# A list scheduler that counts TensorE's instruction blocks and spaces its transfers

## The chip, the cores and the metric

One core of one Trainium2 chip. The metric is the device time of one launch in microseconds, the median of several runs; the kernel before takes 421.56 us (three runs, 420.73 to 422.47).

## The reference, cut to what matters

Attention with a window of 96 keys and 8 global keys, and on its result, transposed to tokens by 512, a feed-forward block with a spatial gate:

```python
scores = scale * np.matmul(q, k.transpose(0, 1, 3, 2))      # 4 x 8 heads, 768 x 768, head size 64
scores = np.where(keep, scores + bias, -1000000000.0)       # bias falls with distance, by head
a = np.exp(scores - np.max(scores, axis=-1, keepdims=True))
attn = np.matmul(a / (np.sum(a, axis=-1, keepdims=True) + 1e-09), v)
...
h = gelu(x @ w_in)                                          # x: 4 x 768 x 512, w_in: 512 x 1024
u, v = h[..., :512], h[..., 512:]
v_n = (v - mu) / np.sqrt(var + 1e-06) * g_ln
v_s = np.einsum('ts,bsd->btd', w_sg, v_n) + b_sg[None, :, None]
out = x + (u * v_s) @ w_out
```

## The kernel before

Attention is cut into 48 units: a batch, a pair of heads, and one of three pairs of 128-query tiles. Of a unit, `score` (L794) multiplies q by the keys in reach in products of 64 x 64 quarters of TensorE, `softmax` takes the minimum on VectorE (L825) and the exponential on ScalarE (L830), and a turn brings the weights to the layout that the product with v needs. For units 0 to 15 the turn is made on TensorE (`turn_quarters`, L929), into two PSUM banks (`tps`) which ScalarE or VectorE copies to `pt` (L937, L938). From unit 16 on VectorE turns blocks of 32 (L893) and two transfers through DRAM do the rest (`far<-tt` L901, four issues; `pt<-far` L905). `weigh` (L959) multiplies by v. A quarter product in float32 is recorded as two passes, so one row of the order with x20 stands for 40 matmuls of the trace.

The feed-forward block works in split float32: a number is the sum of a high and a low part, and each product is three dense matmuls (L466, L467, L468) of 128 x 128 weights by 384 or 512 columns: v tiles (`mm_ps<-win,x`), u tiles (`mm_ps<-x,win`), the spatial mix (`mm_ps<-wsg,z`) and the output (`mm_ps<-gt,wout`). The weights come as 64-bit floats and are split on the fly: a transfer to `stage` (L628), a scaling on ScalarE (L631), bit operations on VectorE (L634, L636, L638), a cast (L641) and a difference (L643). All eight PSUM banks are one pool that scores, turns and dense products share.

What stands in which order on the engines is not written by hand. Every step is recorded as an `Op` with a duration for each engine that can do it, the buffers it uses and the steps it follows. `Plan.search` draws 40 sets of rules and shifts, `Plan.order` walks through time with each of them (an engine that is free takes the first step that is ready, by due time; TensorE by the order in which the code names the steps, up to 40 steps ahead), and the set whose modelled end is earliest is emitted. Every engine then runs its instructions in that order, whatever the real times are. A transfer is modelled as a single wire: it begins 1.3 us after its issue or when the wire is free, takes its bytes, and lands `LANDS` later; no transfer is issued in the plan while the wire is booked more than 1.8 us ahead.

Until 29 us of planned time `keep_on` (L415) puts matmuls on zeros ("fillers") where the plan has TensorE wait for 0.6 us or more.

Of the kernel before, what the change touches and what calls it, by code (L numbers as in the profile page):

```python
# [34 lines left out]
AHEAD = 3  # L35
# [30 lines left out]
PAIRS = 20  # L66
# [29 lines left out]

SLACK = 0.6

LANDS = 1.5

QUEUED = 1.8

# [23 lines left out]
    return "POOL_TS", 0.05 + n / 390 + more, 0.08 + n / 390 + more  # L126


def on_pe(busy, quarters=False):
    return "PE", busy, busy + 0.17, quarters  # L130


class Buf:

    def __init__(self, make, kind=None, spare=0):
        self.spare = spare
# [30 lines left out]
class Op:  # L169
# [2 lines left out]

    def __init__(self, ways, number):
        self.number = number
        self.quarters = ways[0][3] if ways[0][0] == "PE" else None
# [6 lines left out]
        self.ready, self.left, self.due = 0.0, 0, None  # L182


class Now:
# [13 lines left out]
class Plan:  # L199
# [9 lines left out]
    def op(self, ways, reads=(), writes=(), after=()):  # L209
        o = Op(ways, len(self.ops))  # L210
        o.before.update(after)
        for used, put in ((reads, False), (writes, True)):
            for b, part in parts(used):
                o.ready = max(o.ready, b.since)
                for other, at, puts in b.uses:
                    if other is not o and (put or puts) and (None in (part, at) or part == at):
                        o.before.add(other)
                b.uses.append((o, part, put))
                if b not in o.bufs:
                    o.bufs.append(b)  # L220
                    b.ops.append(o)
        self.ops.append(o)
        return o
# [54 lines left out]
    def order(self, start, rules, pace):  # L278
# [7 lines left out]
                b.placed = False  # L286
        free = {e: start.get(e, 0.0) for e in self.ENGINES}
        wire, mode = 0.0, False

        held = {"DVE": 0.0, "POOL": 0.0}  # L290

# [36 lines left out]
        while len(done) < len(self.ops):  # L328
            went = False
            for e in self.ENGINES:  # L330
                if free[e] > t:
                    continue

                short = set()
                can = [o for o in sorted(wait[e], key=pe_at.get if e == "PE" else due)
                       if o.ready <= t and not (o.dma and wire > t + QUEUED)
                       and room(o, e, short)]
                if e == "PE":
                    while head < len(pe) and pe[head].begin is not None:
                        head += 1  # L340
                    can = [o for o in can if pe_at[o] - head <= self.AHEAD]
                    first = pe[head] if head < len(pe) else None
                    if first and first not in can and not first.left and first.ready <= t + 0.12:
                        can = [] if room(first, e, set()) else can
                for o in can:
                    if (e == "SP" and firsts(o) and head < len(pe)
                            and o.due > max(pe[head].due, 0.0) + early):
                        continue
                    way = next(w for w in o.ways if w[0] == e)
                    if begin(way) > t + 0.1:  # L350
                        continue
# [12 lines left out]
                for w in o.ways:  # L364
                    wait[w[0]].remove(o)
                more = 0.0
                if e == "PE":
                    more, mode = self.switch(mode, o.quarters), o.quarters
                    if pace and o.begin > pace[taken] + LAG:
                        return done, math.inf  # L370
                    taken += 1
                free[e] = o.begin + way[1] + more
                o.end = o.begin + way[2] + more
                if way[3]:
                    held[e] = free[e]
                if o.dma:
                    wire = max(wire, t + 1.3) + way[2]
                    o.end = wire + LANDS
                done.append(o)
                for b in firsts(o):  # L380
                    at = places[b.kind]
                    b.slot = min((i for i, x in enumerate(at) if x is not None), key=at.__getitem__)
                    o.since = max(o.since, at[b.slot])
                    at[b.slot], b.placed = None, True
                for b in o.bufs:
                    if b.kind and all(x.begin is not None for x in b.ops):
                        places[b.kind][b.slot] = max(x.end for x in b.ops)
                for x in o.after:
                    x.left -= 1
                    x.ready = max(x.ready, free[e] if e == x.ways[0][0] == "PE" else  # L390
                                  o.end + (SYNC if x.ways[0][0] != e else -0.08))
                    if not x.left:
                        open_for(x)
            if not went:
                nexts = [f for f in [wire - QUEUED, *free.values(), *held.values()] if f > t] + [
                    x + more for at in places.values() for x in at if x is not None
                    for more in (0.0, SLACK) if x + more > t] + [
                    o.ready for e in self.ENGINES for o in wait[e] if o.ready > t]
                if not nexts:
                    return done, math.inf  # L400
                t = min(nexts) + 1e-6
        return done, max(o.end for o in done)

    def keep_on(self, o):

        to = next((b for b in o.bufs if b.kind == "bank" and b.ops[0] is o), None)
        gap = o.begin - o.since
        if to is None or gap < IDLE or o.begin > ON_UNTIL:
            return
        first = o.since == 0.0  # L410

        n = to.ap.shape[1]
        for _ in range(int((gap - 1.0) / (0.000844 * n) if first else
                           (gap - 0.25) / (0.000417 * n + 0.007))):
# [28 lines left out]
class Moe:  # L443
# [13 lines left out]
    def terms(self, n, cols, parts, reads, behind, after, ahead=None):  # L457
# [12 lines left out]
        def add(i):  # L470
            read = reads(i)
            if i == 0:
                read = [r for a in range(n - behind) for r in reads(a)]
            first = self.plan.op([on_pe(3 * cols * 0.000453) + (partial(put, i),)], read, [ps])
            if i == 0 and ahead:
                ahead(first)
            if i == n - 1:
                after(ps)
# [170 lines left out]
def local_global_attention_moe(tc, qk_in, v_in, q_t, k_t, v_n, n_gl, w_in, g_ln, w_sg_t, b_sg,  # L649
# [108 lines left out]

    def bank(name, n, spare=0):
        return Buf(lambda i: pp.tile([P, FF], F32, tag=f"bank{i}", name=name)[:, 0:n], "bank",  # L760
                   spare if scored < PAIRS + AHEAD else min(spare, SPARE_LATE))

    def build_bias(j):
        for h in (2 * j, 2 * j + 1):
# [21 lines left out]
    def score(n, after):  # L786
# [126 lines left out]
    def turn_quarters(n):  # L913
# [19 lines left out]
        turns[:] = [op([on_pe(0.117 * nt, True) + (put,)], ps + [diag], tps)]  # L933
# [7 lines left out]
    def weigh(ns):  # L941
# [56 lines left out]
        first = op([on_pe((0.36 if u == 0 else 0.48) * len(ns), True) + (put,)], used, av)  # L998

        def rest(between):  # L1000

            free = op([(e, 0.06, 0.12, partial(guard, eng)) for e, eng in (
                ("ACT", nc.scalar), ("DVE", nc.vector), ("POOL_TS", nc.gpsimd))], (), (), [first])
            op([on_pe(0.242 * len(ns), True) + (again,)], used, av, between + [free])
            return av

        return first, rest
# [388 lines left out]
```

## Time and profile before

| | |
|---|---|
| median of three runs | 421.56 us (420.73 to 422.47) |
| span of the profiled execution, first to last instruction | 420.1 us |
| TensorE busy | 403.7 us, 96%, 5224 matmuls and 5224 weight loads |
| VectorE / ScalarE / GpSimd busy | 323.5 / 228.2 / 174.6 us |
| TensorE, 5.72 to 57 us: matmuls, share of time busy | 1338, 88% |
| TensorE, 130 to 415 us | 2950, 99.8% |
| instruction transfers (queue 8) | 43, 0.70 MB together |

The page gives the span of the profiled execution and not its device time; the median of the runs stands 1.46 us above that span. A row of the trace gives what an engine ran, how long, and in brackets how long the engine had been idle and what ended that wait. "issue" is a wait that nothing in the profile explains. Busy TensorE is modelled from the starts of matmuls, which overlap.

### The profile page before, as it was taken

The page shows a single profiled execution, that of the slowest core. Times are in us where ns is not written, and L with a number is a line of the kernel's source. Part 1 is how long each engine was busy: PE and PEld are TensorE (multiplying, and loading weights), DVE is VectorE, ACT ScalarE, POOL GpSimd, SP SyncE. Part 2 cuts the span into 40 slices and gives each one's busy share as a digit, 9 for nine tenths or more (in the row PEclk, how much of TensorE's full clock was granted, in tenths as well). Part 3 has the DMA queues.
Part 4 walks back from the last instruction along what each step waited for, and adds up shares of the span by engine and source line. Part 5 has one row for each costly group of instructions (what it writes and reads, how often), then busy time and mean ns, then how long its engine had stood idle before and what let it go on. Part 6 is the DMA issues. An engine that isn't in the chain of part 4 may idle for free.

```text
span 420.1 us, 13632 instructions
## 1 busy us (share of the span) xinstructions
PE 403.7 (96%) x5224; PEld 368.2 (88%) x5224; DVE 323.5 (77%) x1037; ACT 228.2 (54%) x744; POOL 174.6 (42%) x306
## 2 busy tenths in 40 slices
PE   8888989999999999999999999999999999999994
PEld 5766867899998889799999989999999888999994
DVE  6787989999997699995777899885768578754362
ACT  5898889765765765753356556653255343311220
POOL 2234447365686646353554355442553122303100
PEclk9999999989999999999999999999999999999998
DMA  7666575526877778754798785562886521001002
GB/s 246 201 208 166 154 238 153 158 81 173 240 249 255 192 228 238 208 162 114 211 271 227 226 240 141 155 170 54 244 281 172 152 85 39 2 2 48 29 0 81
DMA packets 50040, 68.20 MB, mean 162 GB/s; under 512 B 5809, under 2 KB 33969, under 8 KB 49969
## 3 DMA queue, kind: packets, MB, share of 16 engines
q1 hardware_dynamic: 49968, 67.26, 54.7%
q8 instruction: 43, 0.70, 0.8%
q14 instruction: 29, 0.23, 0.2%
HBM read 48.89 MB, written 18.35 MB: 160 GB/s over the span
## 4 chain that ended last, share of the span: by engine, by line
PE 79%; ACT 6%; DVE 5%; DMA 4%; issue 3%; POOL 1%; SPq 1%; DVEq 0%; POOLq 0%; ACTq 0%
PE mm_ps L466 22%; PE mm_ps L467 21%; PE mm_ps L468 21%; PE s_ps L794 6%; PE av L959 6%; PE tps L929 2%; ACT p L830 2%; DMA pt<-far 2%; DMA qk<-in_qk_in_dram 1%; DMA far<-tt 1%; DVE p L825 1%; DMA v<-in_v_in_dram 1%; ACT stage L631 1%; ACT wsg L641 1%; ACT pt L937 0%
## 5 line engine op out<-in xcount | busy, mean ns | idle before, releaser
L830 ACT ACTIVATE p<-p,pst 128x192 f32<-128x192 f32 (+1 forms) x192 | 84.0, 440 | 36.8 <-DVE pst L825 34.9
L466 PE MATMUL mm_ps<-wsg,z 128*128 128x384 f32 x192 | 65.5, 341 | 0.1
L467 PE MATMUL mm_ps<-wsg,z 128*128 128x384 f32 x192 | 64.9, 338 | 0.0
L468 PE MATMUL mm_ps<-wsg,z 128*128 128x384 f32 x192 | 64.8, 338 | 0.0
L825 DVE CUSTOM_DVE_ANT_0 p<-s_ps,bias 128x192 f32<-128x192 f32 (+1 forms) x192 | 56.5, 337 | 5.1 <-PE s_ps L794 4.9
L851 POOL TENSOR_SCALAR p<-p,pst 128x192 f32<-128x192 f32 (+1 forms) x111 | 50.4, 470 | 15.0 <-DVE pst L843 14.8
L959 PE MATMUL av<-pt,v 64*64 64x128 f32 (+1 forms) x1408 | 47.6, 250 | 1.2 <-DMA pt<-far 1.2
L592 POOL TENSOR_TENSOR o<-o,x 128x384 f32<-128x384 f32 x28 | 28.4, 1013 | 47.5 <-DVE o L589 25.8
L794 PE MATMUL s_ps<-qk 64*64 64x128 f32 (+1 forms) x1408 | 43.1, 249 | 4.1 <-issue 2.5
L794 PEld LDWEIGHTS s_ps<-qk 64*64 64x64 f32 x1408 | 37.1, 134 | 8.9 <-issue 5.7
L466 PE MATMUL mm_ps<-x,win 128*128 128x384 f32 x128 | 44.0, 343 | 0.7 <-ACT pt L937 0.7
L959 PEld LDWEIGHTS av<-pt,v 64*64 64x64 f32 x1408 | 37.2, 134 | 8.2 <-issue 4.9
L468 PE MATMUL mm_ps<-gt,wout 128*128 128x384 f32 x128 | 43.1, 336 | 0.1
L466 PE MATMUL mm_ps<-gt,wout 128*128 128x384 f32 x128 | 43.1, 337 | 0.0
L467 PE MATMUL mm_ps<-gt,wout 128*128 128x384 f32 x128 | 42.9, 335 | 0.0
L468 PE MATMUL mm_ps<-x,win 128*128 128x384 f32 x128 | 42.9, 335 | 0.0
L467 PE MATMUL mm_ps<-x,win 128*128 128x384 f32 x128 | 42.9, 335 | 0.0
L466 PE MATMUL mm_ps<-win,x 128*128 128x512 f32 x96 | 39.6, 412 | 0.0
L500 ACT CAST gt<-y 128x384 fp32r<-128x384 f32 x27 | 13.8, 511 | 46.2 <-DVE y L561 33.4
L467 PE MATMUL mm_ps<-win,x 128*128 128x512 f32 x96 | 37.7, 393 | 0.0
L468 PE MATMUL mm_ps<-win,x 128*128 128x512 f32 x96 | 37.6, 392 | 0.0
L466 PEld LDWEIGHTS mm_ps<-wsg,z 128*128 128x128 f32 x192 | 36.5, 190 | 1.1 <-issue 0.5
(109 smaller groups left out, 905.2 us busy)
## 6 DMA issues: line engine op xcount, KB each, us to landing
qk<-in_qk_in_dram SPq DMA_DIRECT2D x32, 352.0 KB, 3.9
far<-tt SPq DMA_DIRECT2D x96, 96.0 KB, 2.6
pt<-far SPq DMA_DIRECT2D x24, 384.0 KB, 3.9
v<-in_v_in_dram SPq DMA_DIRECT2D x32, 256.0 KB, 3.7
out_dram<-o SPq DMA_DIRECT2D x32, 192.0 KB, 2.7
qk<-in_qk_in_dram SPq DMA_DIRECT2D x16, 288.0 KB, 3.8
v<-in_v_in_dram SPq DMA_DIRECT2D x16, 192.0 KB, 3.6
far<-tt SPq DMA_DIRECT2D x32, 80.0 KB, 2.2
```

What stands on the lines that cost most here:

```text
L466: mm(ps.ap, ah, bh, start=(i == 0), stop=False)
L467: mm(ps.ap, ah, bl, start=False, stop=False)
L468: mm(ps.ap, al, bh, start=False, stop=(i == n - 1))
L500: put(out[:, 0, :], src.ap)
L592: lo = lambda eng: eng.tensor_tensor(o.ap, o.ap, xm[:, 1, :].bitcast(F32), ALU.add)
L631: op([on_act(n, 0.07) + (lambda: nc.scalar.mul(f.ap, words()[:, :, 1].bitcast(F32), 2.0 ** -112),)], [raw], [f])
L794: nc.tensor.matmul(s_ps[h][e * HQ:(e + 1) * HQ, i * W + c0:i * W + c0 + n], qk[rows, qc:qc + HQ], qk[rows, QW + k0:QW + k0 + n], start=Tru ...
L825: nc.vector.tensor_tensor_reduce(out=p[:, g, 0:nk], in0=s_ps[h][:, i * W:i * W + nk], in1=bias[:, 2 * j + h, w0:w0 + nk], op0=ALU.add, op1 ...
L830: op([on_act(nk, 0.225) + (lambda p=p, g=g, nk=nk, i=i: nc.scalar.activation(p[:, g, 0:nk], p[:, g, 0:nk], AF.Exp, bias=st[:, 0, i, g:g + ...
L851: op([on_pool_ts(nk, -0.10) + (partial(scaled, lambda o, a, c: nc.gpsimd.tensor_scalar(o, a, c, 1.0, ALU.mult, ALU.mult)),), on_act(nk, 0. ...
L929: nc.tensor.matmul(tps[r][g * HQ:(g + 1) * HQ, a * HQ:(a + 1) * HQ], pc[rows, c:c + HQ], diag[rows, 2 * i + c // W], start=True, stop=True)
L959: nc.tensor.matmul(to, v[rows, vc:vc + D], of, stop=True, skip_group_check=True, **kw)
```

## The change

The planner alone is changed; no step of the computation is.

- `on_pe` is given the number of products of a step, and each step counts its instruction words (two a product, four for quarter products, which have two passes).
- `order` has a new function `stall`. It counts words. At word 194 and every 256 words from there TensorE enters a block; the next block can be entered 4.6 us after the one before was, or after its own fetch began, and a step that crosses the edge too early is made longer by the difference. Fillers are counted as words too, as many as `zeros`, which `keep_on` now shares, says.
- A transfer books 0.25 us more of the wire (`EACH`) and lands 0.75 us after its bytes (`LANDS`) and no longer 1.5 us.

```diff
-LANDS = 1.5
+LANDS = 0.75
+EACH = 0.25
+BLOCK, FIRST_BLOCK, FETCH = 256, 194, 4.6
...
-def on_pe(busy, quarters=False):
-    return "PE", busy, busy + 0.17, quarters
+def on_pe(busy, products, quarters=False):
+    return "PE", busy, busy + 0.17, quarters, (4 if quarters else 2) * products
...
+        read, entered, fetched = 0, 0.0, 0.0
+        def stall(at, n, busy):
+            nonlocal read, entered, fetched
+            late, edge = 0.0, (read - FIRST_BLOCK) // BLOCK * BLOCK + BLOCK + FIRST_BLOCK
+            while edge <= read + n:
+                entered = at + late + (edge - read) / max(n, 1) * busy
+                late += max(fetched - entered, 0.0)
+                fetched, edge = max(entered, fetched) + FETCH, edge + BLOCK
+            read += n
+            return late
...
                 if e == "PE":
+                    zeros = self.zeros(o) if firsts(o) else 0
+                    stall(o.begin, 2 * zeros, 0.0)
                     more, mode = self.switch(mode, o.quarters), o.quarters
+                    more += stall(o.begin + more, o.words + 0.3, way[1])
...
-                    wire = max(wire, t + 1.3) + way[2]
+                    wire = max(wire, t + 1.3) + way[2] + EACH
                     o.end = wire + LANDS
...
-        return op([on_pe(0.56 if u == 0 else 0.67, True) + (put,)], [qk], s_ps, after + turns)
+        return op([on_pe(0.56 if u == 0 else 0.67, 12 if u == 0 else 16, True) + (put,)], [qk], s_ps, after + turns)
```

With other modelled times the planner arrives at another order on every engine up to the last units; from there the TensorE rows run alike. Fillers go from 72 to 63: 11 ahead of the first scores, then 27, 10, 11, 8 and 5 in five places; now 10, then 30, 15 and 8 in three. Lines below `order` stand 25 lines lower in the new kernel (L929 is L954, L794 is L819, L631 is L656, L641 is L666, L937 is L962).

TensorE at the last of the sixteen turns, before: `tps` are the banks of the turn, `s_ps` those of the scores of a later unit.

```order
L468 MATMUL mm_ps<-wsg,z 128x384
L959 MATMUL av<-pt,v 64x128 x4
L959 MATMUL av<-pt,v 64x64 x4
L929 MATMUL tps<-diag,p 64x64 x20
L794 MATMUL s_ps<-qk 64x128 x4
L794 MATMUL s_ps<-qk 64x64 x4
L794 MATMUL s_ps<-qk 64x128 x4
```

The same turn now; of the 15 dense products that follow it the first three are shown.

```order
L493 MATMUL mm_ps<-wsg,z 128x384
L954 MATMUL tps<-diag,p 64x64 x20
L491 MATMUL mm_ps<-x,win 128x384
L492 MATMUL mm_ps<-x,win 128x384
L493 MATMUL mm_ps<-x,win 128x384
```

The scores stood right behind the turn; now 15 dense products stand between. The scores and the 13th of those products wait for a bank that ScalarE frees.

ScalarE at the same place, before: `stage` rows are the scaling of weights (the last two of the three in a row are of w_out, which a transfer brings), `pt<-tps` the two copies that free the banks of the last turn.

```order
L631 ACTIVATE stage<-stage 128x256 x3
L641 CAST win<-stage 128x256
L937 COPY pt<-tps 128x5x64
L500 CAST z<-vg 128x512
L485 ACTIVATE u<-mm_ps 128x384
L937 COPY pt<-tps 128x5x64
```

And now:

```order
L656 ACTIVATE stage<-stage 128x256
L855 ACTIVATE p,pst<-p,pst 128x192 x2
L666 CAST win<-stage 128x256 x3
L510 ACTIVATE u<-mm_ps 128x384
L855 ACTIVATE p,pst<-p,pst 128x192
L962 COPY pt<-tps 128x5x64
L656 ACTIVATE stage<-stage 128x256
L666 CAST wout<-stage 128x256
L962 COPY pt<-tps 128x5x64
```

One instruction stood between the second scaling of w_out and the first copy; now seven do, and a third scaling stands between the two copies.

SyncE's queue of transfers that brings those weights, before:

```order
L628 DMA stage<-in_w_in_dram 128x512 x3
L628 DMA stage<-in_w_out_dram 128x512
L784 DMA v<-in_v_in_dram 128x384
L777 DMA qk<-in_qk_in_dram 128x704
L628 DMA stage<-in_w_out_dram 128x512 x3
```

And now:

```order
L653 DMA stage<-in_w_in_dram 128x512 x3
L649 DMA stage<-in_w_sg_t_dram 128x384
L809 DMA v<-in_v_in_dram 128x384
L802 DMA qk<-in_qk_in_dram 128x704
L653 DMA stage<-in_w_out_dram 128x512 x4
```

The first two transfers of w_out had two of a unit's loads between them; now four of w_out stand in a row behind those loads.

More of the change, by code (lines that the diff above doesn't have):

```diff
@@ L126, in on_pool_ts, with __init__ @@
     return "POOL_TS", 0.05 + n / 390 + more, 0.08 + n / 390 + more
-def on_pe(busy, quarters=False):
-    return "PE", busy, busy + 0.17, quarters
+def on_pe(busy, products, quarters=False):
+    return "PE", busy, busy + 0.17, quarters, (4 if quarters else 2) * products
 class Buf:
-    def __init__(self, make, kind=None, spare=0):
-        self.spare = spare
+    def __init__(self, make, kind=None, spare=0, wide=0):
+        self.spare, self.wide = spare, wide
         self.make, self.kind, self.uses, self.ops, self.tile = make, kind, [], [], None
@@ L174, in __init__ @@
         self.number = number
-        self.quarters = ways[0][3] if ways[0][0] == "PE" else None
+        self.quarters, self.words = ways[0][3:5] if ways[0][0] == "PE" else (None, 0)
         self.ways = [(w[0].split("_")[0], w[1], w[2], w[0] in ("DVE_SB", "POOL"), w[-1])
@@ L181, in __init__ @@
         self.begin = self.end = None
-        self.ready, self.left, self.due = 0.0, 0, None
+        self.ready, self.left, self.due, self.banks = 0.0, 0, None, 0
 class Now:
@@ L219, in op @@
                 if b not in o.bufs:
+                    if b.kind == "bank" and not b.ops and not o.banks:
+                        o.banks = b.wide
                     o.bufs.append(b)
@@ L402, in order, with zeros @@
         return done, max(o.end for o in done)
+    @staticmethod
+    def zeros(o):
+        gap, n = o.begin - o.since, o.banks
+        if not n or gap < IDLE or o.begin > ON_UNTIL:
+            return 0
+        return int((gap - 1.0) / (0.000844 * n) if o.since == 0.0 else
+                   (gap - 0.25) / (0.000417 * n + 0.007))
     def keep_on(self, o):
         to = next((b for b in o.bufs if b.kind == "bank" and b.ops[0] is o), None)
[L407 to L414, printed above, removed]
+        n = o.banks
+        for _ in range(self.zeros(o)):
             self.tc.nc.tensor.matmul(to[:, 0:n], self.on[:, 0:P], self.on[:, 0:n], start=True,
@@ L473, in add @@
                 read = [r for a in range(n - behind) for r in reads(a)]
-            first = self.plan.op([on_pe(3 * cols * 0.000453) + (partial(put, i),)], read, [ps])
+            first = self.plan.op([on_pe(3 * cols * 0.000453, 3) + (partial(put, i),)], read, [ps])
             if i == 0 and ahead:
@@ L760, in bank @@
         return Buf(lambda i: pp.tile([P, FF], F32, tag=f"bank{i}", name=name)[:, 0:n], "bank",
-                   spare if scored < PAIRS + AHEAD else min(spare, SPARE_LATE))
+                   spare if scored < PAIRS + AHEAD else min(spare, SPARE_LATE), n)
     def build_bias(j):
@@ L931, in put @@
                                          start=True, stop=True)
-        turns[:] = [op([on_pe(0.117 * nt, True) + (put,)], ps + [diag], tps)]
+        turns[:] = [op([on_pe(0.117 * nt, 4 * nt, True) + (put,)], ps + [diag], tps)]
         for r in range(2):
@@ L997, in weigh @@
         ends, used = [], [x for v, pt, _ in todo for x in (v, pt)]
-        first = op([on_pe((0.36 if u == 0 else 0.48) * len(ns), True) + (put,)], used, av)
+        first = op([on_pe((0.36 if u == 0 else 0.48) * len(ns), (8 if u == 0 else 12) * len(ns), True) + (put,)], used, av)
         def rest(between):
@@ L1003, in rest @@
                 ("ACT", nc.scalar), ("DVE", nc.vector), ("POOL_TS", nc.gpsimd))], (), (), [first])
-            op([on_pe(0.242 * len(ns), True) + (again,)], used, av, between + [free])
+            op([on_pe(0.242 * len(ns), 4 * len(ns), True) + (again,)], used, av, between + [free])
             return av
```

## The prediction

> **What bounds the kernel now.** I began with the stretches, to see where TensorE has slack. Columns: busy us (instructions) of TensorE's matmuls, its weight loads, VectorE, ScalarE, GpSimd; then granted clock, DMA share, GB/s.
>
> ```profile
> 5.72:30.00 24.28, 21.34 (x634) 16.84 (x638) 20.21 (x94) 21.81 (x83) 6.34 (x11) 1.00 0.73 245
> 30.00:57.00 27.00, 23.79 (x704) 18.98 (x697) 22.62 (x90) 22.98 (x84) 12.24 (x24) 1.00 0.59 164
> 57.00:86.00 29.00, 26.65 (x473) 22.83 (x474) 27.55 (x90) 25.36 (x85) 12.84 (x20) 1.00 0.54 164
> 86.00:130.00 44.00, 43.14 (x446) 40.86 (x446) 40.35 (x120) 27.10 (x86) 29.22 (x44) 0.96 0.68 201
> 130.00:415.00 285.00, 284.38 (x2950) 266.55 (x2946) 209.75 (x637) 129.43 (x407) 111.52 (x193) 1.00 0.52 150
> ```
>
> From 130 us to the last matmul TensorE idles 285.00 - 284.38 = 0.62 us. It is the bound there, its products are the same in any order, and the orders run alike late. So the change can only pay by what TensorE loses before 130 us: every microsecond that it waits there moves the whole rest. The waits of TensorE by who ended them:
>
> ```profile
> PE s_ps L794 <- issue: 2.5, 2, 1.3
> PE tps L929 <- issue: 2.0, 3, 0.9
> PE s_ps L794 <- ACT pt L937: 1.5, 1, 1.5
> PE av L959 <- DMA pt<-far: 1.2, 2, 0.8
> PE tps L929 <- POOL diag L861: 0.9, 1, 0.9
> PE mm_ps L466 <- ACT pt L937: 0.7, 1, 0.7
> ```
>
> The largest share, 2.5 + 2.0 = 4.5 us, is "issue": no engine and no transfer is waited for. The chain shows when:
>
> ```profile
> 13.72 1.17 issue
> ...
> 23.97 0.53 issue
> 28.08 0.60 issue
> 38.09 0.90 issue
> 55.70 1.29 issue
> ```
>
> Between the starts of these waits (and of a short one at 47.12 us) the stretches count:
>
> ```profile
> 13.72:23.97 10.25, 8.84 (x253) 6.80 (x252) 8.53 (x39) 9.01 (x39) 3.91 (x6) 1.00 0.61 189
> 23.97:28.08 4.11, 3.58 (x127) 2.79 (x127) 3.15 (x12) 3.72 (x13) 0.73 (x2) 1.00 0.56 179
> 28.08:38.09 10.01, 8.47 (x254) 6.79 (x253) 7.74 (x32) 8.47 (x33) 4.19 (x9) 1.00 0.69 191
> 38.09:47.12 9.03, 8.13 (x255) 6.57 (x253) 7.76 (x30) 7.69 (x29) 3.73 (x9) 1.00 0.47 124
> 47.12:55.70 8.58, 8.50 (x254) 6.92 (x253) 8.32 (x33) 7.44 (x31) 4.08 (x7) 1.00 0.59 181
> ```
>
> This is the reading that matters: 253 matmuls and 252 loads, then 127 and 127, then 254 and 253. The waits lie 254 instructions apart or twice that, whatever was run. With the few instructions of the sequencer that the counts leave out, these are blocks of 256, and the instruction queue agrees:
>
> ```profile
> q8 instruction: 43, 0.70, 0.8%
> ```
>
> 10,448 matmuls and loads in 43 transfers are 243 each. Nine blocks took 10.25 + 4.11 + 10.01 + 9.03 + 8.58 = 41.98 us, 4.66 us each; the change plans 4.6. So from 13 to 57 us TensorE is paced by its instructions: a block of small quarter products is used up about as fast as the next arrives.
>
> The second place is the wait of 1.5 us for a copy of ScalarE. ScalarE's own rows around it:
>
> ```profile
> 79.89 0.79 ACT L631 ACTIVATE stage<-stage 128x256 f32<-128x256 f32 x2
> 82.36 0.45 ACT L631 ACTIVATE stage<-stage 128x256 f32<-128x256 f32 x1 [1.67 <-DMA stage<-in_w_out_dram]
> 83.85 0.41 ACT L641 CAST win<-stage 128x256 fp32r<-128x256 f32 x1 [1.04 <-DVE stage L638]
> 84.16 0.42 ACT L937 COPY pt<-tps 128x320 f32<-128x320 f32 x1
> ```
>
> ScalarE stood behind a weight that had not landed (1.67 us), then behind VectorE (1.04 us), with the copy that frees the bank queued behind both. TensorE stood at the scores that needed the bank:
>
> ```profile
> 82.70 0.40 PE L794 MATMUL s_ps<-qk 64*64 64x128 f32 x3
> 84.63 0.77 PE L794 MATMUL s_ps<-qk 64*64 64x128 f32 x24 [1.53 <-ACT pt L937]
> ```
>
> And it cost more than the wait, as stretches of 3.41 us show:
>
> ```profile
> 83.14:86.55 3.41, 1.80 (x40) 1.56 (x41) 3.34 (x12) 2.65 (x8) 1.48 (x2) 1.00 0.00 0
> 86.55:89.97 3.42, 3.42 (x13) 3.42 (x12) 3.42 (x15) 2.61 (x11) 1.40 (x2) 0.50 0.25 84
> 89.97:93.38 3.41, 3.41 (x21) 3.41 (x21) 3.38 (x9) 1.07 (x5) 3.39 (x5) 1.00 0.25 83
> ```
>
> After a stretch that was busy for 1.80 of 3.41 us the granted clock is 0.50 for 3.42 us; half of that, 1.71 us, is lost on dense products.
>
> **The change part by part.** *The block model* removes no fetch. It tells the planner that the stalls come, so that the other engines' steps are laid beside them. Its own gain in the paced stretch is small, since the pace of 4.66 us holds in any order with as many instructions: 9 fewer fillers, one of them ahead of the first scores, are 8 x 2 = 16 words, 16/256 of a block, 0.29 us. I take -0.3. The bounds: nothing, if the saved words fall where a block waits for data anyway; and 9 x (4.66 - 4.11) = 4.95 us, if every block ran like the fastest above. I stay near nothing, because the nine already average what the planner now expects. Dense products of a few v tiles fill the blocks as before.
>
> Here a rule speaks against the change. The Trainium skill, "Runtime: NRT & Kernel Launch", section "Instruction fetch mechanics", has blocks of 256 instructions prefetched while the current one runs, and the crossing "mostly hidden". The trace agrees on the blocks and not on the cost (waits of 0.53 to 1.29 us at the edges); by the rule this term would be 0, and the forecast 419.0 instead of 418.7.
>
> *The order at the last turn.* The scores now stand 15 dense products behind the turn. A dense product takes 3.41/21 = 0.16 us in the last stretch above. The 13th needs a bank as well, so the cover is 12 x 0.16 = 1.9 us, against the 1.53 us that was missing. ScalarE has seven instructions between the second scaling of w_out and the copy, where it had one, so a late weight has time to land. I take both losses as gone: -1.53 - 1.71 = -3.24 us. What is late next is the second copy, behind a third scaling of w_out; if that holds it, the price is the row of 0.7 us above, once. Bounds of this part: 0 and -3.24, or -3.94 if the other wait of 0.7 goes too.
>
> *The transfers.* SyncE's rows for the loads of q and k give from issue to landing:
>
> ```profile
> DMA to landing us min/median/max: 2.7/3.9/6.3
> ```
>
> Their 360 KB (128 x 704 x 4 bytes) book 1.0 us in the plan, so the old plan had 1.3 + 1.0 + 1.5 = 3.8 us alone and the new one 3.3; the fastest landed in 2.7. Both are inside the rows, but a plan that expects data sooner puts its user sooner, and every engine's queue runs in order. Where it shows is the product with v behind `pt<-far` (TensorE queued behind it): now 1.2 us in 2 waits, among 32 such loads. I take half as much again, +0.6; the bounds are -1.2 (both gone) and +1.2 (doubled). SyncE passes the same number of issues; its own work hides it.
>
> *Sum* against the profiled span of 420.1 us: -0.3 - 3.24 + 0.6 = -2.9, to 417.2. The page gives no device time for that execution; the median of the runs stands 1.46 us above its span, which I carry over: 421.56 - 2.9 = **418.7 us**. About 0.5%, 2.1 us, is what a measurement of this kernel can tell from no change.
>
> **The rivals.**
> *The wait moves.* ScalarE and VectorE are 25.36 and 27.55 of 29 us busy from 57 to 86 us, so there is little slack, and another copy may come late there. For it: 20 weight chunks are still to come, each with steps that wait for it (count, min/median/max ns of an issue, first and last start in us):
>
> ```profile
> L628 SPq DMA_DIRECT2D stage<-in_w_out_dram x8: 327/328/516, 76.5 to 104.8; - x8
> L624 SPq DMA_DIRECT2D stage<-in_w_sg_t_dram x12: 328/338/974, 58.5 to 125.4; - x12
> ```
>
> Then 3.24 us come back elsewhere, in a wait and half a clock: -0.3 + 0.6 = +0.3, about 421.9.
>
> *Two such waits, slower.* Before, fillers stood in five places after the first scores and now in three (30, 15 and 8 of them). If the banks at the last turn come over 1.9 us after it and a second stretch of 3.41 us, in the first 57 us where fillers went, is idle by over 1.6 us, there are two events of 3.24 us where there was one: 421.56 + 3.24 = 424.8. Against it: with waits up to 1.29 us no stretch up to 57 us lost its clock.
>
> *The clock drops anyway.* The Trainium skill, "TensorE: Matmul & The Clock Gate", section "Part 1: The HAM clock gate", lets the clock fall after an idle window of about 3.4 us, which a gap of 1.53 us is not. As a mechanism here: the drop at 86.55 us has another cause than the wait and comes again, 1.71 us stay, and 418.7 + 1.7 = 420.4. Against it: it follows the one stretch that was barely half busy.
>
> *A better pace.* If the waits for data in the paced stretch now fall inside the fetches, half of the 4.95 us bound is gained: 418.7 - 2.4 = 416.3. For it: a wait of 0.9 us for `diag` stands beside, not inside, a stall; against it: the fetch itself.
>
> **How the numbers follow.** Forecast 0.45 (within 417.2 and 420.2; four in five of it over 0.5% faster: 0.36, and 0.09 the same); wait moves 0.22 (0.20 the same, 0.02 slower); two waits 0.10 slower; clock anyway 0.08 the same; better pace 0.15 faster. Faster 0.36 + 0.15 = 0.51, the same 0.09 + 0.20 + 0.08 = 0.37, slower 0.12. The range reaches from just under the better pace, 416.0, to 423.3, the moved wait with the transfers' upper bound (421.9 + 0.6) and the spread of the runs, 0.8; it leaves out the two waits, 0.10, and the tails of the others.
>
> **What would show it.** Right: no granted clock of 0.50 between 80 and 100 us; the "pt L937" wait under 0.7 us; waits of "issue" still about 4 us and 254 or 508 instructions apart. The transfers' term is right if the waits on `pt<-far` sum to 1 to 2.4 us. Wrong: idle or a halved clock at another place before 130 us, or a stretch from 13 to 57 us that is paced by data and not by blocks; and if TensorE after 130 us idles more than 2 us, I looked in the wrong stage.

## The result and the profile after

| | before | after |
|---|---|---|
| median of 20 runs each | 421.27 us (418.63 to 424.96) | 425.16 us (421.88 to 428.85) |
| ratio, 95% interval | | 1.0081 (1.0052 to 1.0111) |
| span of the profiled execution | 420.1 us | 425.8 us (that run took 427.55) |

By the medians the changed kernel is slower by 3.9 us, by the ratio 0.8%, and it lies outside the predicted range. The ratios here and below leave out single runs more than 1.5% above the fastest of their kernel, so they differ a little from the ratios of the medians. The profiled spans differ by 5.7 us, more than the medians, since the execution profiled lies high among its runs; a second and a third profile of the changed kernel have spans of 426.1 and 424.0 us, a second one of the kernel before 420.6.

The stretches of the changed kernel, columns as in the prediction:

```profile
5.72:30.00 24.28, 19.93 (x565) 16.55 (x557) 20.52 (x90) 20.03 (x75) 3.05 (x6) 0.93 0.72 236
30.00:57.00 27.00, 25.16 (x778) 20.33 (x779) 23.30 (x98) 22.60 (x85) 10.50 (x19) 1.00 0.59 173
57.00:86.00 29.00, 25.78 (x363) 21.40 (x363) 26.38 (x89) 23.06 (x77) 11.93 (x17) 0.94 0.53 161
86.00:130.00 44.00, 42.46 (x475) 39.14 (x473) 41.04 (x132) 29.97 (x98) 22.80 (x33) 1.00 0.59 184
130.00:420.00 290.00, 288.40 (x3020) 269.30 (x3019) 219.76 (x671) 122.57 (x388) 109.36 (x191) 1.00 0.53 151
```

The halved clock is gone from 86 to 130 us (0.96 before, 1.00 now) and has appeared ahead of 30 us (0.93) and between 57 and 86 us (0.94). Around both places, in stretches of 3.41 us:

```profile
12.66:16.07 3.41, 1.28 (x64) 1.04 (x59) 3.30 (x13) 2.56 (x10) 0.62 (x1) 1.00 0.71 256
16.08:19.49 3.41, 3.41 (x96) 3.41 (x99) 2.13 (x12) 2.71 (x11) 0.00 (x0) 0.50 0.42 120
57.04:60.45 3.41, 1.28 (x6) 0.97 (x6) 3.33 (x13) 2.25 (x11) 1.54 (x3) 1.00 0.28 97
60.45:63.86 3.41, 3.41 (x75) 2.67 (x78) 1.74 (x7) 1.83 (x8) 1.39 (x2) 0.50 0.67 199
```

Each half clock (a stretch at a granted clock of 0.50) follows a stretch in which TensorE was busy 1.28 of 3.41 us. Some of TensorE's waits over the whole span (us in total, times, longest):

```profile
PE av L984 <- issue: 2.8, 1, 2.8
PE av L984 <- DMA pt<-far: 2.3, 4, 1.1
PE s_ps L819 <- issue: 2.1, 1, 2.1
PE av L984 <- ACT pt L962: 1.8, 2, 1.3
...
PE s_ps L819 <- DVE vg L515: 0.6, 1, 0.6
...
PE mm_ps L491 <- ACT pt L962: 0.4, 1, 0.4
```

Two waits of "issue", 2.1 and 2.8 us, at 13.94 and 56.33 us: the first block edge (an edge is where TensorE passes from one block of 256 instructions to the next), and the one nine blocks on. Before, the waits at these two edges were 1.17 and 1.29 us. At the last turn only the last two rows quoted are left, 0.6 and 0.4 us, where 0.7 and 1.5 us were.

How the difference divides, in wide stretches; before:

```profile
5.72:110.00 104.28, 95.78 (x1986) 81.98 (x1990) 93.05 (x339) 84.86 (x296) 45.58 (x71) 0.98 0.61 184
110.00:180.00 70.00, 68.77 (x892) 61.28 (x885) 60.61 (x204) 46.25 (x154) 42.46 (x74) 1.00 0.76 225
180.00:415.00 235.00, 234.75 (x2325) 222.79 (x2323) 166.81 (x487) 95.57 (x293) 84.12 (x145) 1.00 0.48 136
```

And after:

```profile
5.72:110.00 104.28, 94.85 (x1967) 80.28 (x1960) 93.22 (x343) 82.12 (x286) 37.94 (x58) 0.97 0.56 176
110.00:180.00 70.00, 67.00 (x878) 58.35 (x877) 61.21 (x216) 44.19 (x153) 36.02 (x62) 1.00 0.79 234
180.00:420.00 240.00, 239.88 (x2356) 228.09 (x2354) 176.57 (x518) 91.92 (x281) 83.68 (x146) 1.00 0.47 134
```

Up to 110 us TensorE idles 9.43 us now and 8.50 before: 0.9 more. From 110 to 180 us it idles 3.00 us and not 1.23: 1.8 more. After 180 us it never waits; the 0.12 and 0.25 us there lie behind the last matmul, which ends at 419.88 us now and at 414.75 before. What follows the last matmul takes 5.9 us in this profile and 5.3 before: 0.6 more. Two stretches of half clock for one are at most 1.7 us more, and perhaps less: the one at 16.08 us still passed 96 matmuls, where the paced stretches before passed 253 in 10.25 us, that is 84 in 3.41. So idle time and clock give at most 5.0 of the 5.7 us.

Counting the work done by a given time places the loss better. Dense products (tile `mm_ps`: busy us (count), clock, DMA share, GB/s), before:

```profile
0.00:110.00 110.00, 50.04 (x237) 0.98 0.61 182
110.00:180.00 70.00, 54.28 (x272) 1.00 0.76 225
180.00:420.00 240.00, 207.17 (x1125) 1.00 0.47 135
```

And after:

```profile
0.00:110.00 110.00, 48.22 (x226) 0.97 0.56 175
110.00:180.00 70.00, 51.73 (x254) 1.00 0.79 234
```

The changed kernel is 11 dense products behind at 110 us and loses 18 more by 180 us. At 207.17/1125 = 0.184 us each that is an estimate of 2.0 and 3.3 us; of the small products both have done the same number by 180 us, fillers aside. The first part is there early: at the end of the wait at 56.33 us both kernels have done 36 dense products and 1360 or 1361 matmuls in all, the one before at 56.99 us and the changed one at 59.17, 2.2 us later. In its other two profiles the changed kernel passes that edge at 61.29 and 59.89 us and is 15 and 8 dense products behind at 110 us. So the loss has two pieces of some size, one that stands at that edge and a larger one between 110 and 180 us.

### The profile page after: what moved, and what is told of

The parts are those of the page before. It is cut to its first block, busy times and chain, and to the rows that moved or that the text cites. A ratio compares the mean times of both kernels' runs of the same rounds, so it can differ in the third digit from the quotient of the medians.

```text
span 425.8 us, 13608 instructions
## 1 busy us (share of the span) xinstructions
PE 406.0 (95%) x5215; PEld 368.9 (87%) x5215; DVE 334.2 (78%) x1085; ACT 219.7 (52%) x720; POOL 160.1 (38%) x282
## 4 chain that ended last, share of the span: by engine, by line
PE 71%; DVE 15%; DMA 6%; issue 4%; SPq 1%; POOL 1%; ACT 1%; DVEq 0%; POOLq 0%; ACTq 0%
PE mm_ps L491 19%; PE mm_ps L492 18%; PE mm_ps L493 18%; PE av L984 6%; PE s_ps L819 6%; DMA pt<-far 2%; DVE p L850 2%; PE tps L954 2%; DVE stage L661 2%; DMA far<-tt 2%; DVE stage L663 2%; DMA qk<-in_qk_in_dram 1%; DVE win L668 1%; PE tps L440 1%; DVE tt L918 1%
## 5 line engine op out<-in xcount | busy, mean ns | idle before, releaser
L984 PE MATMUL av<-pt,v 64*64 64x128 f32 (+1 forms) x1408 | 49.3, 254 | 7.7 <-issue 2.8
L876 POOL TENSOR_SCALAR p<-p,pst 128x192 f32<-128x192 f32 (+1 forms) x104 | 47.3, 471 | 23.0 <-DVE pst L868 22.4
L984 PEld LDWEIGHTS av<-pt,v 64*64 64x64 f32 x1408 | 38.5, 137 | 16.0 <-issue 7.8
L819 PE MATMUL s_ps<-qk 64*64 64x128 f32 (+1 forms) x1408 | 44.0, 254 | 3.0 <-issue 2.1
L819 PEld LDWEIGHTS s_ps<-qk 64*64 64x64 f32 x1408 | 38.3, 137 | 8.2 <-issue 5.5
L864 POOL TENSOR_SCALAR pst<-pst 128x4 f32<-128x4 f32 x42 | 10.7, 255 | 80.4 <-ACT p L855 77.1
L510 ACT ACTIVATE u<-mm_ps 128x384 f32<-128x384 f32 x32 | 15.6, 487 | 44.8 <-PE mm_ps L493 44.0
```

Source lines behind the costliest of these rows:

```text
L510: op([on_act(n) + (lambda: nc.scalar.activation(out.ap, h.ap, AF.Square, scale=math.sqrt(GELU_C * GELU_A)),)], [h], [out])
L819: nc.tensor.matmul(s_ps[h][e * HQ:(e + 1) * HQ, i * W + c0:i * W + c0 + n], qk[rows, qc:qc + HQ], qk[rows, QW + k0:QW + k0 + n], start=Tru ...
L864: ("POOL_TS", 0.24, 0.28, lambda: nc.gpsimd.tensor_scalar(sums(1), sums(1), 1e-9, None, ALU.add)),
L876: op([on_pool_ts(nk, -0.10) + (partial(scaled, lambda o, a, c: nc.gpsimd.tensor_scalar(o, a, c, 1.0, ALU.mult, ALU.mult)),), on_act(nk, 0. ...
L984: nc.tensor.matmul(to, v[rows, vc:vc + D], of, stop=True, skip_group_check=True, **kw)
```

## The experiments

My first theory was that the new order sets transfers across the two block edges, that the long fetches there halve the clock, and that this is the loss. The rivals: one half of the change does it (the transfers' new times, or the block model); or neither, and any other order of this planner is as slow.

### Each half alone

`dma_only` is the kernel before with the transfers' times, `block_only` the changed kernel without them.

```diff
-LANDS = 1.5
+LANDS = 0.75
-                    wire = max(wire, t + 1.3) + way[2]
+                    wire = max(wire, t + 1.3) + way[2] + 0.25
```

```diff
-LANDS = 0.75
-EACH = 0.25
+LANDS = 1.5
+EACH = 0.0
```

> The kernel before with the two numbers of the transfers alone (0.75 us to land, 0.25 us more of the wire each), without the block model. Three theories. Fetch: the loss comes from block edges that the new order puts behind rows of weight transfers (a wait of 2.8 us where there was 1.3). Transfers: it comes from data planned sooner than it lands, which the product with v waits for after 95 us. Draw: neither part has an effect of its own; any change of a modelled time makes the planner take another of its forty draws, and draws differ by about 1%. Transfers expects 424 us or more here, with 2 us or more of waits on pt<-far. Fetch expects 421 us with waits of issue near 4.5 us, none over 1.5. Draw expects anything from 418 to 426 and waits at places of its own.

> The changed kernel with the old numbers of the transfers (1.5 us to land, nothing added to the wire): the block model alone. Fetch expects 424 us or more and a wait of issue over 2 us; Transfers expects 421 us or less, with waits on pt<-far of 1.2 us or less; Draw expects anything from 418 to 426, and the differences of the two parts from before not to add up to the 3.9 us of the whole change.

Measured: 1.0069 (1.0032 to 1.0106) and 1.0115 (1.0069 to 1.0160) of the kernel before. The theory of the fetch had its expectation met by `block_only` and missed by `dma_only`. The theory of the transfers expected 2 us or more of waits on `pt<-far` in the first and 1.2 or less in the second; they were 1.7 and 2.0. Either half loses, and the two losses, 0.69% and 1.15%, add up to 1.84% and not to the 0.81% of the whole change. As the cost of one half, or as the sum of two costs, the result can't be read. Each of the three is another order. Both halves have a long wait of "issue" in their profiles; of `dma_only` first, then of `block_only`, whose profiled execution was its slowest of six:

```profile
PE s_ps L794 <- issue: 3.8, 1, 3.8
```

```profile
PE av L984 <- issue: 3.8, 1, 3.8
```

### Other draws of the same planner

The search draws 40 sets of rules from a seeded generator. Another seed gives other sets and so another order, with the model untouched. This was done for both kernels, with seeds 2, 3 and 4.

```diff
-        rnd = random.Random(1)
+        rnd = random.Random(2)
```

> The kernel before with seed 2 for 1; the old model. Fetch and Transfers expect it within 1 us of the kernel before, since nothing of the model has changed. Draw expects a difference of 2 us or more either way.

> The changed kernel with another seed of the planner's random draws, 2 for 1; the model is the same. Fetch and Transfers, which hold the model to blame, expect it slower than the kernel before by 2 to 5 us again. Draw expects that it can as well come out level or faster, and that it differs from the changed kernel by over 2 us.

> The old model with seed 3. Draw, now the leading theory, expects the kernel before to be a lucky draw: this one slower by 2 to 6 us, like seed 2 (1.0114). A theory that the old order is good because its model is good expects it level with the kernel before, and seed 2 the exception.

> The old model with seed 4: as for seed 3, 2 to 6 us slower by Draw. If one of the two is level with the kernel before and one slower by over 2 us, the spread of the draws is as wide as the whole change.

> The new model with seed 3. Draw expects it anywhere from 0 to 6 us over the kernel before. That the new model is the better one, seed for seed, expects the three new draws of seeds 2, 3 and 4 to be faster in the mean than the three old ones by over 1 us (seed 2: 1.0066 against 1.0114); that it is worse expects the reverse.

> The new model with seed 4: as for seed 3, anywhere from 0 to 6 us over the kernel before by Draw; in the mean of seeds 2 to 4 under the old model's by over 1 us if the new model is the better one.

| seed | old model | new model |
|---|---|---|
| 1 | 1 (the kernel before) | 1.0081 (1.0052 to 1.0111) |
| 2 | 1.0114 (1.0064 to 1.0164) | 1.0066 (1.0030 to 1.0102) |
| 3 | 1.0125 (1.0082 to 1.0168) | 1.0150 (1.0100 to 1.0201) |
| 4 | 1.0116 (1.0070 to 1.0162) | 1.0047 (1.0018 to 1.0077) |

This is the experiment that decides. With the old model untouched, every other draw costs 1.1 to 1.3%, by the middle of the intervals more than the change did (the intervals overlap). The kernel before is a draw that stands 1.2% ahead of its own planner's other three, and any change that makes the planner draw anew gives that up. Single results fit the other theories as well: `after_seed2` came out 2 to 5 us slower, as they expected, and within 1 us of the changed kernel, where the theory of the draw had expected over 2 us between them. It is `before_seed2` to `before_seed4` that only the draw explains.

Whether the new model is better as a model stays open. Over seeds 2, 3 and 4 it is ahead, 1.0088 against 1.0118 on average, about 1.3 us, which is over the 1 us set ahead of those runs; over all four seeds the two are level, 1.0086 and 1.0089, and the four new draws alone are spread over 1%.

The draws also speak on the half clock. `before_seed2` and `before_seed4` show none after the start (mean granted clock 0.999 and 0.997 in the profiled executions, 0.993 in the kernel before), and they are 1.1% slower all the same. So the halved clock is not what slow orders have in common. The profile of `before_seed2` in the wide stretches:

```profile
5.72:110.00 104.28, 93.56 (x1998) 78.56 (x1997) 92.54 (x347) 80.52 (x280) 37.51 (x58) 1.00 0.56 181
110.00:180.00 70.00, 68.19 (x891) 60.29 (x890) 63.51 (x221) 43.74 (x155) 34.62 (x58) 1.00 0.75 225
```

At full clock TensorE idles 10.72 us up to 110 us, 2.2 more than in the kernel before, and 1.81 us up to 180 us, 0.6 more. Its dense products are 218 up to 110 us, 19 fewer than in the kernel before, and 267 from there to 180 us, 5 fewer. So this order loses mostly before 110 us, and the changed kernel mostly after: the place of the loss goes with the draw.

### Two orders in one kernel

To find the place of the loss, one order was used up to 90 us of planned time and the other from there: `splice_ba` begins with the order before, `splice_ab` with the new one.

```diff
+FIRST, SECOND, CUT = (1.5, 0.0, False), (0.75, 0.25, True), 90.0
...
+        head = [o for o in first if how[o][0] < CUT]
+        inside = set(head)
+        todo = head + [o for o in second if o not in inside]
```

> A spliced order: what the old planner places before 90 us of its plan in the old order, all the rest in the order of the changed kernel. TensorE's rows are those of the kernel before up to row 425 of 2639 and those of the changed kernel from there but for a seam. By the profiles, counted against the same work, the changed kernel loses 1.5 us more up to 90 us and 3.6 us more from there to 180. Early (the fetch waits and half clocks of the first 65 us make the loss) expects about 421.5. Late (waits on pt<-far, on VectorE and on ScalarE from 95 to 180 us make it) expects 425. Draw in its strong form, that a place has nothing to do with it, expects no rule.

> The other splice: the changed kernel's order to 90 us of its plan, then the old order. Early expects 425, Late 422. If the two splices together lose about what the whole change loses (3.9 us), the loss has its place; if both are slower than the kernel before by the whole, a seam costs by itself and the splices say nothing.

Measured: 1.0132 (1.0075 to 1.0189) and 1.0179 (1.0106 to 1.0252). By the ratios both are slower than either whole order (the intervals of both reach into the changed kernel's, 1.0052 to 1.0111), so a seam seems to cost by itself. That is the case in which, as expected, the place of the loss can't be read from them. The profile of `splice_ba` shows one such cost, a wait for ScalarE's queue, of a length that no profile of either whole order has:

```profile
PE av L1028 <- ACTq L1057: 3.2, 1, 3.2
```

### What a block costs

`blocks_alone` leaves all of the computation out: 1280 quarter products on one unit's q and k, 40 loads of 256 KB, and 16 stores of zeros, 384 KB each, as the output. The transfers were meant for the second half and ran at the start, so the first part is the loaded one. `after_again` is the changed kernel unchanged, for a second profile.

```diff
+        products(QUIET)
...
+        for r in range(ROWS):
...
+            nc.sync.dma_start(t, v_in[r % B, r // B % NPAIR, 1])
...
+        products(BUSY)
```

> Not the task's computation: 1280 quarter products alone (64 columns, each two passes of a load and a matmul, so 5120 instructions, 20 blocks), the first half with no transfer under way, the second with 40 loads of 256 KB from SyncE in a row; the output is left at zero. Fetch expects the first half to be paced at the change's 4.6 us a block or a little under (4.0 to 4.3, as the fastest in the kernel), and the second half slower and uneven, 5 to 7 us a block. The rule that crossings are mostly hidden expects about 2 us a block in both halves, 127 matmuls of 15 to 17 ns.

> The changed kernel once more, for a second profile. Fetch expects a wait of issue of over 2 us near 56 us again. If a long wait stands at another edge or nowhere, and half clocks too, then they come and go from run to run, and the one profile's 2.8 us is no fixed part of the loss.

The stretches of `blocks_alone` (VectorE and GpSimd idle; columns TensorE, its loads, VectorE, GpSimd, clock, DMA share, GB/s):

```profile
14.44:42.52 28.08, 15.88 (x637) 15.24 (x640) 0.00 (x0) 0.00 (x0) 0.71 1.03 388
46.59:86.19 39.60, 22.42 (x1381) 20.94 (x1377) 0.00 (x0) 0.00 (x0) 1.00 0.05 13
```

And what TensorE waited for:

```profile
PE s_ps L694 <- issue: 35.7, 19, 4.7
```

At 127 matmuls a block, 1381 of them in 39.60 us are 3.64 us a block beside 13 GB/s of transfers, and 637 in 28.08 us are 5.60 us a block beside 388 GB/s. The loaded part also ran at a granted clock of 0.71, so not all of the 1.96 us need be the fetch's; TensorE's idle time alone is 2.43 us a block there and 1.58 in the quiet part. The planner's 4.6 us and my 4.66 lie between the two conditions. The trace's records of the packets on queue 8 (16 KB, one a block) show where the difference arises: a packet takes about 1 us in both parts, but it begins 1.0 to 1.4 us after the wait ahead of it has ended in the quiet part, and 2.4 to 4.3 us after it in the loaded part. `after_again` repeats the picture of the changed kernel, with the waits at the two edges 3.40 and 2.88 us long.

The prediction weighed the Trainium skill, "Runtime: NRT & Kernel Launch", section "Instruction fetch mechanics", by which the crossing is mostly hidden. Here it is not: 19 waits hold 35.7 us, 1.9 us each on average.

### The transfers held back at the two edges

In the changed kernel's SyncE rows a row of three 256 KB weights is issued just ahead of the wait at 56.33 us:

```profile
53.19 1.37 SPq L653 DMA_DIRECT2D stage<-in_w_in_dram  x3
```

`hold_rows` has the changed kernel's order, with this row waiting for a product just ahead of the edge, so that the fetch is first in line; `hold_both` also holds one of two 512 KB weights until TensorE is past the first edge. `before_again` and `after_third` are the two kernels unchanged, profiled on the same chip; the longest "issue" wait of `before_again` is 1.64 us.

```diff
+HOLD = ((450, "loads"), (2690, "rows"))
...
+            late = [loads[2]] if late == "loads" else rows[:3]
...
+            at = todo.index(o) + 1
+            todo[at:at] = late
```

> The changed kernel with its order on TensorE, VectorE, ScalarE and GpSimd. In SyncE's queue the second of two 512 KB loads of w_in in a row is moved behind one load of q and k, and waits until TensorE is past the first edge; the row of three 256 KB loads before the edge near 56 us waits for a product just ahead of it. Fetch expects the two long waits (2.1 to 3.4 us at 14, 2.8 at 56) to fall to 1.5 us or less each, and the time by 2 to 4 us, to 421 to 423. If the waits fall and the time does not, they were not what the time hung on. If they stay, the transfers do not make them.

> The changed kernel with only the row of three 256 KB loads held until a product just ahead of the edge near 56 us; SyncE's order is unchanged too. Fetch expects the wait there to fall from 2.8 to 1.5 us or less, the one near 14 us to stay, and the time to fall by 1 to 3 us.

> The kernel before once more, for a second profile. If the order makes the short waits, its longest wait of issue is under 1.6 us again; if the run does, it can be over 2.

> The changed kernel a third time. If the order makes the long waits, two of over 2 us stand near 14 and 57 us again.

TensorE's rows at the two edges, in `after_third`, the changed kernel on the same chip (start, us, instruction, in brackets the wait ahead of it):

```profile
17.05 0.43 PE L819 MATMUL s_ps<-qk 64*64 64x128 f32 x9 [3.30 <-issue]
...
59.89 0.38 PE L984 MATMUL av<-pt,v 64*64 64x128 f32 x2 [2.52 <-issue]
```

With the row of three held (`hold_rows`):

```profile
16.22 0.69 PE L853 MATMUL s_ps<-qk 64*64 64x128 f32 x9 [2.26 <-issue]
...
57.96 0.38 PE L1018 MATMUL av<-pt,v 64*64 64x128 f32 x2 [1.42 <-issue]
```

With both held (`hold_both`), where the second edge shows no wait:

```profile
14.83 0.43 PE L853 MATMUL s_ps<-qk 64*64 64x128 f32 x9 [0.81 <-issue]
20.03 1.60 PE L853 MATMUL s_ps<-qk 64*64 64x128 f32 x30 [2.72 <-ACT xh L1115]
31.84 0.68 PE L1018 MATMUL av<-pt,v 64*64 64x128 f32 x24 [2.26 <-ACT xh L1115]
```

So the transfers under way do make the long fetch waits, as expected, though each held order has one profile only: with its transfers held, the second edge shows 1.42 us or none, where three profiles of the changed kernel show 2.84, 2.88 and 2.52, and the first 0.81 us, where they show 2.13, 3.40 and 3.30. In the packet records the fetch for the second edge begins at 55.38 us in `hold_rows` and at 56.85 in the changed kernel, and takes about 1 us in both. The expected gain of 1 to 4 us didn't come: 1.0076 (1.0046 to 1.0107) for `hold_rows`, level with the changed kernel, and 1.0111 (1.0064 to 1.0158) for `hold_both`. In `hold_both` the held weight is late in its turn, in ScalarE's row:

```profile
19.17 0.66 ACT L690 ACTIVATE stage<-stage 128x512 f32<-128x512 f32 x1 [4.09 <-DMA stage<-in_w_in_dram]
```

and TensorE waits 2.72 and 2.26 us for ScalarE, in the last two rows above. In `hold_rows` TensorE still idles from 110 to 180 us, 4.11 us by its stretch:

```profile
110.00:180.00 70.00, 65.89 (x873) 57.55 (x872) 59.54 (x208) 42.20 (x146) 36.98 (x63) 1.00 0.79 229
```

Its dense products, in the stretches used above:

```profile
0.00:110.00 110.00, 49.92 (x236) 0.98 0.57 179
110.00:180.00 70.00, 50.56 (x249) 1.00 0.79 229
```

At 110 us `hold_rows` is, in this profile, one dense product short of the kernel before, where the changed kernel was 8 to 15 short, so the shorter wait seems to have paid up to there; from 110 to 180 us it is 23 short, and the gain is gone. My first theory falls in its second half: the long fetches are made by the order and are real, but the whole time does not hang on them alone.

`before_again` settles one more point. The wait at the last turn recurs, and no half clock follows. That profile's half clock follows the edge wait of 1.64 us at 54.78 us instead, and its span is 420.6 us all the same:

```profile
85.23 0.77 PE L794 MATMUL s_ps<-qk 64*64 64x128 f32 x24 [1.51 <-ACT pt L937]
```

```profile
81.76:85.17 3.41, 1.96 (x64) 1.47 (x62) 3.24 (x12) 1.18 (x4) 1.32 (x2) 1.00 0.05 17
85.17:88.59 3.42, 3.24 (x48) 3.00 (x49) 3.38 (x14) 3.37 (x13) 1.35 (x1) 1.00 0.01 2
54.45:57.87 3.42, 1.78 (x29) 1.34 (x21) 2.04 (x11) 2.21 (x6) 2.00 (x3) 1.00 0.62 208
57.87:61.28 3.41, 3.41 (x75) 2.67 (x78) 2.71 (x10) 2.18 (x11) 0.92 (x2) 0.50 0.81 214
```

## Why the prediction was wrong

**The step that failed** is the sum itself: it took the order before, took one wait out, and carried all the rest over as if the new order had the same losses. The words are "since the pace of 4.66 us holds in any order with as many instructions" and "the orders run alike late". The pace held only between the edges: nine blocks from the wait at 13.94 us to the one at 56.33 took 42.39 us, 4.71 each. The waits at those two edges went from 1.17 and 1.29 us to 2.13 and 2.84, and TensorE passed the second 2.2 us later. Late, the orders don't run alike: from 110 to 180 us the changed kernel does 254 dense products and not 272. There was no term for a new order; four draws of the new model put it at +0.5 to +1.5%, three of the old at +1.1 to +1.3%. None of my rivals had this: they were one or two events at named places, and the loss is that of a draw.

One reading was off as well: of the 0.62 us that I took as idle time from 130 us to the last matmul, 0.25 lie behind the last matmul. Up to it TensorE idles 0.4 us from 130 us on before, and 1.5, 2.6 and 1.8 us in the three profiles of the changed kernel. My sign for the wrong stage was over 2 us, and one of the three shows it.

**The block model, -0.3.** Mis-sized and of the wrong sign as a bound: my ends were 0 and -4.95 us, both gains, and the changed kernel stands 2.2 us behind at the ninth edge. The time of a block is not a constant of the instructions: alone, blocks took 3.64 us beside little traffic and 5.60 beside much. The sign that I had named, waits of "issue" of about 4 us, reads 4.9, but in two long waits and not in five.

**The last turn, -3.24.** The wait went as forecast (0.4 for the copy, 0.6 for VectorE, no half clock between 80 and 100 us). But only the wait of 1.53 us belonged to that place. The 1.71 us of clock were not tied to it: in the second profile of before the wait stayed and the drop came elsewhere. My rival "the clock drops anyway" comes nearest, and it deserved more than 0.08; it named another cause at the same place, while the runs show the same kind of cause, a poorly used stretch, at another place. In the changed kernel the drop came twice in the first and third profiles and over three stretches in the second.

**The transfers, +0.6.** Right in kind: the waits on `pt<-far` are 2.3 us in this profile, 1.1 and 1.6 us in the other two of the changed kernel, against 1.2 and 0.3 us. That is inside the bounds. They also lie in the stretch from 110 to 180 us, where the larger piece of the loss stands, but they are only a part of it. In this window the waits of the changed kernel are

```profile
PE av L984 <- DMA pt<-far: 2.3, 4, 1.1
PE mm_ps L492 <- DVE gt L529: 0.4, 1, 0.4
PE mm_ps L492 <- DVE wsg L668: 0.3, 1, 0.3
```

and those before one row, the 1.2 us on `pt<-far` that the prediction quotes.

**The rival "two such waits", 424.8 us,** names the time almost to the microsecond, and that is luck. It placed one wait with its half clock at the last turn and one ahead of 57 us where fillers went. The changed kernel has no such wait at the last turn; its two half clocks follow block edges, the idle time comes from longer fetches and not from fillers, and orders with no half clock are as slow.

**What stays open.** Why seed 1 of the old model is 1.2% ahead of the others isn't shown; no edge, clock or wait that I could take away gave the time back. What makes the changed kernel lose about 3 us from 110 to 180 us wasn't tried; its idle time accounts for 1.8 of them.

## What to carry to other kernels

Changing a list scheduler's costs redraws the whole order. Where the order at hand stands ahead of its planner's other draws, as here, a redraw has a price of its own, here 0.5 to 1.5%; measure it with a few seeds of both models before crediting or blaming the model. An order that is faster than its planner's other draws is a draw to keep: save the order, and judge a new model by the mean of its draws. A wait that is taken out of one place is a gain only if the rest of the order stays, and a local gain of 0.4% doesn't outweigh a spread of 1%. To find where an order loses, count the work done by a given time: idle time alone left part of the loss without a place.

## What the runs showed of the hardware

In `blocks_alone` quarter products use up a block of 256 instructions faster than the next arrives even beside 13 GB/s of transfers (2.06 us of matmuls in 3.64 us a block, 22.42/10.9), and transfers make it worse: 5.60 us a block, with a longest wait of 4.7 us, partly at a lower clock. In `dma_only` and `block_only` one edge wait reached 3.8 us. A packet of the fetch takes about 1 us either way; what grows is the time until it begins.

The clock follows a grid of 3.413 us: in each profile the changes of the granted clock lie a whole number of such stretches apart (16.08 and 60.45 us in the changed kernel, 13 stretches). Taken on that grid, the eighteen profiles together have 19 stretches at full clock in which TensorE was busy for 1.47 us or less, and a half clock follows each; no half clock follows a stretch that was busy for 1.86 us or more; between 1.50 and 1.80 us it follows 7 of 16. (The stretches after the last products are left out.) So it matters how a wait falls on the grid. The edge wait of 2.84 us in the first profile of the changed kernel left a stretch of 1.28 us, and a half clock followed. The one of 2.88 us in the second profile falls across two stretches, and none followed:

```profile
56.81:60.23 3.42, 1.60 (x78) 1.35 (x75) 2.40 (x13) 3.31 (x12) 1.59 (x3) 1.00 0.83 282
60.23:63.64 3.41, 2.35 (x32) 1.64 (x34) 2.68 (x14) 2.20 (x9) 1.83 (x3) 1.00 0.33 74
```

The drop of the kernel before moved from 86.55 us in one profile to 57.87 in the other. One wait and the half clock next to it are therefore two terms, with two chances.
